# Attention's first 24 steps: where a unit of maxima stands in a step, and the queue of four early pairs of rows

## The chip, the cores and the metric

The kernel runs on one core of a Trainium2 chip. The metric is the time of one execution on the device, in microseconds. A core has five engines with an instruction queue each, which run in order and wait for each other through semaphores: TensorE (PE, matrix products; its weight loads are shown as PEld), VectorE (DVE), ScalarE (ACT), GpSimd (POOL) and SyncE (SP, which here only issues transfers). ACT and POOL can issue transfers too, from the same in-order queue that holds their arithmetic. [...]

## What is computed

Three stages follow each other: an attention in which a query sees only the keys of its own cluster, a dense layer pair, and a layer of eight experts. The change touches only the first:

```
q_assign = argmax(q_n . c_n)          # cluster of each query (and of each key, k_assign)
mask     = q_assign[:, None] == k_assign[None, :]
scores   = where(mask, scale * q @ k.T, -1e9)
scores   = scores - max(scores, axis=-1)
attn     = exp(scores) / (sum(exp(scores)) + 1e-9)
out      = attn @ v                   # batch 2, heads 8, sequence 768, head size 64
```

The heads are taken two at a time, so there are 8 pairs, numbered i from 0 to 7.

## The kernel before, in words

**Steps.** A pair of heads is 12 steps, in two halves r of 384 queries; there are 96 steps, called s0 to s95 here. `plan` (line 481) puts down for each step which functions are due in it, and `advance` (line 637) writes a step's instructions out. The order in which they are written is the order in each engine's queue.

**What a step holds.** `score` (line 385) makes the transposed scores of 128 keys and 384 queries for both heads: four matmuls on PE (lines 395 and 398) into one of two large PSUM tiles, then the exponential on ACT (line 402), which writes P. `pv` (line 418) multiplies the step before's P with the values: four matmuls (line 428). `add_up` (line 405) adds that P to a running sum on POOL, two additions (line 416). P has four buffers.

**Units of maxima.** The row maximum must be known before a half's scores are made. A unit (`max_unit`, line 355) is two matmuls of 96 rows (line 365) into a large PSUM tile and one reduction on DVE (line 369). A half of a pair has six units, 12 a pair: units 6 to 11 belong to pair 0's second half, 12 to 17 to pair 1's first, and so on. `RAMP` (line 552) places the early ones: steps 7, 9, 11, 17 and 20 have two units (14 and 15, 17 and 18, 20 and 21, 26 and 27, 30 and 31), steps 4 and 14 have none, and the others have one, as have all from step 24 on.

**The two large tiles.** `big` hands out two PSUM tiles in turn, to scores and units in the order in which they are written. A matmul into one of them waits until the instruction that read it last is through: the exponential of a score or the reduction of a unit.

**The small banks.** `misc` hands out three banks in turn to transposes of q and k (`split`, line 233), similarities to the centroids (`sims`, line 251), one-hot transposes (line 277), `first` (line 291), the sums (`norm1`, line 441), transposed maxima (`max_put`, line 374) and a part of the weights' narrowing (line 712). The bank of the sums is read last by `norm2`, one step after `norm1`, on DVE (line 456).

**max_put.** When a half's six units are done, `max_put` (line 371) transposes the maxima on PE, copies them on ACT (line 376, tile mt) and sends them with two transfers of 1.5 KB, one a head, into row 96 of QA, which the second matmul of `score` (line 398) reads. The pair of transfers is issued by SP, but for 0 < 2 i + r < 5, that is for the halves (0,1), (1,0), (1,1) and (2,0), by ACT (line 378). They are due in steps 4, 10, 14 and 20 and are needed by the scores of steps 6, 12, 18 and 24.

**The order within a step.** The first unit of the step comes ahead of all; then what was left late by the step before on DVE; then score, norm1, pv, add_up, onehot_t and first; then the rest (max_put, norm2 and norm3, split, sims, pick, spreads and loads on SP, narrowing); and last the step's second unit, if it has one:

```
for a in units[:1]:
    self.max_unit(*a)
```

With norm2, in the rest, POOL multiplies (line 455), DVE makes rs (line 456), ACT shifts it (line 464) and POOL multiplies again (line 465). norm1 of the halves (0,0), (0,1) and (1,0) is due in steps 8, 14 and 20, norm2 in steps 9, 15 and 21.

Of the kernel before, what the change touches and what calls it, by code (L numbers as in the profile page):

```python
# [23 lines left out]
def f32(ap):  # L24
    return ap.bitcast(F32)
# [144 lines left out]
class Attention:  # L170
# [200 lines left out]
    def max_put(self, i, r):  # L371
        nc, K, st = self.nc, self.K, self.st[i]
        pt = K.misc("pmt") if i + r else K.bank("a", "pmt")
        nc.tensor.transpose(pt[:, 0:128], self.mx[r], K.ident)
        mt = self.p.tile([6, 128], F32R, tag="mt", name="mt")
        nc.scalar.activation(out=mt, in_=pt[0:6, 0:128], func=AF.Copy, scale=-1.0)
        QA = self.QA[i % 3]
        e = nc.scalar if 0 < 2 * i + r < 5 else nc.sync
        for h in range(2):
            e.dma_start(  # L380
                out=f32(QA[96:97, h, 384 * r:384 * r + 384].rearrange("a (t p) -> a t p", t=3)),
                in_=f32(mt[3 * h:3 * h + 3, :]),
            )
# [97 lines left out]
    def plan(self, N):  # L481
# [5 lines left out]
        def at(s, f, *a):  # L487
            if s >= 0:
                steps.setdefault(s, []).append((f, a))
# [12 lines left out]
        for i in range(NP):  # L502
# [28 lines left out]
            if i:  # L531
                for j, kind in enumerate(("ql", "qu", "kb", "kl")):
                    for h in range(2):
                        at(max(12 * i - 12, 3) + self.BS * j, self.spread, i, (kind, h))
            if i:
# [8 lines left out]
                at(s, N.load, c + 3)  # L544
        return steps

    BS = 2
    SOON, SLOTS = (14, 19, 22), (0, 2, 7, 8, 10)
    B2 = 0

# [79 lines left out]
    def begin(self, C, Z, N):  # L630
        self.start(C, Z, N)
        self.steps = self.plan(N)
        self.late = []
        self.at = min(self.steps)
        self.end = max(self.steps) + 2

    def advance(self, upto, more={}):

        for s in range(self.at, upto):
            todo = self.steps.get(s, [])  # L640
            units = [a for f, a in todo if f == self.max_unit]
            first = [a for f, a in todo if f == self.max_put and a == (0, 1)]
            for a in units[:1]:
                self.max_unit(*a)
            for a in first:
                self.max_put(*a)
            for g in self.late:
                g()
            for g in more.get(s, []):
                g()  # L650
            now = (self.score, self.norm1, self.pv, self.add_up, self.onehot_t, self.first)
            todo = [x for f in now for x in todo if x[0] == f] + [x for x in todo if x[0] not in now]
            late = [f(*a) for f, a in todo if f != self.max_unit and not (f == self.max_put and a in first)]
            for a in units[1:]:
                self.max_unit(*a)
            self.late = [g for g in late if callable(g)]
        self.at = upto

# [1076 lines left out]
```

## Time and profile before

| | us |
|---|---|
| median of 3 runs | 788.06 (787.91 to 789.1) |
| the profiled execution | 787.98 |
| its span, first to last instruction | 786.1 |
| around the span | 1.9 |
| TensorE busy | 753.6 (96%) |
| VectorE busy | 588.8 (75%) |
| ScalarE busy | 466.6 (59%) |
| GpSimd busy | 220.7 (28%) |

Busy counts instructions that compute. An engine that issues a transfer is not counted as busy while it does so, and a matmul's end is modelled, so a row's start is surer than its end. Steps are recognised by the starts of line 395: s4 starts at 37.01 us, s5 at 40.81, s6 at 43.68, s7 at 46.43, s8 at 50.39, s9 at 53.19, s10 at 56.77, s11 at 59.47, s12 at 63.40, s14 at 67.73, s15 at 71.71, s16 at 74.78, s17 at 77.54, s18 at 81.51, s20 at 86.03, s21 at 90.16, s22 at 92.71 and s24 at 97.38.

### The profile page before, as it was taken

What the parts mean: (1) busy time and instruction counts of PE and PEld (TensorE: products, weight loads), DVE (VectorE), ACT (ScalarE), POOL (GpSimd) and SP (SyncE); (2) the same over time, 40 slices, a digit from 0 to 9 for tenths busy, and PEclk for the clock granted to TensorE, in tenths of its full rate; (3) what the DMA queues carried; (4) which work ended last, traced back from release to release, by engine and by line L of the source; (5) the groups of instructions that cost most, each with busy time, mean ns of one, the idle gap of its engine ahead of it and who ended that gap; (6) DMA issues with size and microseconds to landing.
All of it is one profiled execution on the core that took longest, in us unless ns stands there. A gap on an engine that the chain in (4) does not pass through costs nothing.

```text
span 786.1 us, 12515 instructions
## 1 busy us (share of the span) xinstructions
PE 753.6 (96%) x4295; PEld 607.5 (77%) x4297; DVE 588.8 (75%) x1195; ACT 466.6 (59%) x901; POOL 220.7 (28%) x247
## 2 busy tenths in 40 slices
PE   8989999999999989899999999999999999999994
PEld 5656566666654568788989899999888999999993
DVE  6756778879779799999997688788677665666661
ACT  4445778778776766555556454445645655656651
POOL 6256668787792200010000030000231101101110
PEclk9999999999999999999999999999999999999998
DMA  9696698989793539796465456232429867986640
GB/s 200 146 218 132 164 273 249 230 237 250 202 281 120 214 128 341 256 317 229 178 233 182 140 188 196 108 141 74 135 82 282 267 213 215 276 262 222 199 125 22
DMA packets 118694, 155.78 MB, mean 198 GB/s; under 512 B 35006, under 2 KB 82206, under 8 KB 114528
## 3 DMA queue, kind: packets, MB, share of 16 engines
q1 hardware_dynamic: 113952, 131.82, 57.6%
q0 software_dynamic: 4624, 23.09, 7.4%
q8 instruction: 36, 0.59, 0.3%
q14 instruction: 34, 0.28, 0.1%
q10 hardware_dynamic: 48, 0.01, 0.0%
HBM read 93.65 MB, written 42.24 MB: 173 GB/s over the span
## 4 chain that ended last, share of the span: by engine, by line
PE 70%; DVE 16%; issue 5%; ACT 4%; DMA 3%; POOL 1%; SPq 1%; ACTq 0%; POOLq 0%; DVEq 0%
PE ph L852 12%; PE o L913 11%; PE he L1509 9%; PE y L1542 9%; PE acc L428 6%; PE pm L365 4%; PE pst L395 3%; PE pst L398 3%; PE psim L251 3%; DVE m L369 2%; DVE n L867 2%; DVE cut L810 1%; DMA n<-in_moe_w_in_dram 1%; ACT r L877 1%; PE o L1161 1%
## 5 line engine op out<-in xcount | busy, mean ns | idle before, releaser
L810 DVE TENSOR_TENSOR cut<-raw,cut 128x512 fp32r<-128x512 f32 x168 | 110.1, 686 | 26.6 <-ACT cut L809 17.6
L369 DVE TENSOR_REDUCE m<-pm 128x1 f32<-128x768 f32 x96 | 91.0, 954 | 49.3 <-PE pm L365 48.9
L416 POOL TENSOR_TENSOR sum<-sum,P 128x384 f32<-128x384 f32 x104 | 104.3, 1034 | 13.1 <-ACT P L402 10.9
L402 ACT ACTIVATE P<-pst 128x768 f32<-128x768 f32 x96 | 77.7, 809 | 43.2 <-PE pst L398 40.4
L809 ACT ACTIVATE cut<-raw 128x512 fp32r<-128x512 f32 x168 | 98.1, 623 | 2.0 <-DMA raw<-in_moe_w_dram 2.0
L1542 PE MATMUL y<-cut,hy 128*128 128x512 f32 x384 | 99.3, 394 | 0.0
L1509 PE MATMUL he<-xeh,cut 128*128 128x256 f32 x512 | 92.5, 280 | 0.2 <-ACT xeh L1463 0.2
L877 ACT ACTIVATE r<-n,two 128x384 f32<-128x384 f32 x64 | 39.5, 617 | 81.1 <-DVE n L867 80.1
L1509 PEld LDWEIGHTS he<-xeh,cut 128*128 128x128 f32 x512 | 82.2, 188 | 5.5 <-ACT xeh L1463 0.4
L428 PE MATMUL acc<-P,vn 128*64 128x384 f32 x384 | 82.4, 508 | 0.1
L1542 PEld LDWEIGHTS y<-cut,hy 128*128 128x128 f32 x384 | 67.6, 188 | 10.9
L852 PE MATMUL ph<-xh,cut 128*128 128x384 f32 x256 | 67.1, 343 | 5.8 <-DVE t L889 3.5
L1509 PE MATMUL he<-xel,cut 128*128 128x256 f32 x256 | 71.5, 279 | 0.2 <-DVE xel L1464 0.2
L395 PE MATMUL pst<-QB,KB 128*128 128x384 f32 x192 | 67.1, 349 | 4.7 <-DVE m L369 3.5
L1514 ACT ACTIVATE hy<-he 128x256 fp32r<-128x256 f32 x64 | 24.5, 383 | 71.7 <-PE he L1509 71.7
L1554 POOL DMA_INDIRECT out_dram<-ye,meta x17 | 18.3, 1077 | 171.6 <-ACT ye L1552 156.9
L852 PE MATMUL ph<-xh,again 128*128 128x384 f32 x256 | 66.1, 339 | 0.0
L398 PE MATMUL pst<-QA,KA 97*128 97x384 f32 x192 | 64.9, 338 | 0.0
L913 PE MATMUL o<-cut,gh 128*128 128x512 f32 x192 | 59.8, 392 | 1.0 <-DVE rs L456 1.0
L1515 DVE SCALAR_TENSOR_TENSOR hy<-he,hy 128x256 fp32r<-128x256 f32 x64 | 27.1, 423 | 44.7 <-ACT hy L1514 44.7
L913 PE MATMUL o<-again,gh 128*128 128x512 f32 x192 | 59.6, 392 | 0.0
L365 PE MATMUL pm<-KA,QA 96*128 96x384 f32 x192 | 54.1, 369 | 2.8 <-DVE m L369 2.7
(238 smaller groups left out, 1616.1 us busy)
## 6 DMA issues: line engine op xcount, KB each, us to landing
raw<-in_moe_w_dram SPq DMA_DIRECT2D x72, 256.0 KB
raw<-in_moe_w_dram SPq DMA_DIRECT2D x36, 512.0 KB
kept<-cut POOLq DMA_DIRECT2D x16, 1024.0 KB, 8.5
again<-kept SPq DMA_DIRECT2D x16, 1024.0 KB
n<-in_moe_w_in_dram SPq DMA_DIRECT2D x16, 512.0 KB
n<-in_moe_w_out_dram SPq DMA_DIRECT2D x16, 512.0 KB
wf<-n SPq DMA_DIRECT2D x32, 256.0 KB
raw<-wf SPq DMA_DIRECT2D x16, 512.0 KB
```

The source lines that it names most:

```text
L365: nc.tensor.matmul(ps[:, g, 0:384], lhsT=QA[0:96, h, q0:q0 + 128], rhs=KA[0:96, h, 384 * g:384 * g + 384], start=True, stop=True,)
L369: nc.vector.reduce_max(out=self.mx[r][:, 3 * h + t:3 * h + t + 1], in_=ps[:, :, 0:384], axis=AX.XY)
L395: nc.tensor.matmul(ps[:, h, 0:384], lhsT=KB[:, h, ks], rhs=QB[:, h, qs], start=True, stop=False)
L398: nc.tensor.matmul(ps[:, h, 0:384], lhsT=KA[0:97, h, ks], rhs=QA[0:97, h, qs], start=False, stop=True)
L416: e.tensor_add(out=o[:, h], in0=a[:, h], in1=b[:, h])
L428: nc.tensor.matmul(acc[64 * h:64 * h + 64, 0:384], lhsT=st["v"][:, h, t, :], rhs=pt[:, h, :], start=(t == 0), stop=(t == self.NK - 1),)
L809: nc.scalar.activation(out=t[:, 0, part], in_=raw[:, part], func=AF.Copy)
L810: self.low.tensor_sub(out=t[:, 1, part], in0=raw[:, part], in1=f32(t[:, 0, part]))
L852: nc.tensor.matmul(ps[:, 0:384], lhsT=w[:, k, :], rhs=x[:, k, sl], start=(k == 0 and j == 0), stop=(k == 3 and j == 2),)
L913: nc.tensor.matmul(self.acc[t], lhsT=g[:, c], rhs=w, start=(f == 0 and j == 0), stop=(f == self.NF - 1 and j == 2),)
L1509: nc.tensor.matmul(ps[:, 0:MAIN], lhsT=w[:, k, :], rhs=x[:, k, :], start=(k == 0 and j == 0), stop=(k == 3 and j == 2),)
L1542: nc.tensor.matmul(st["y"][s], lhsT=g[:, c], rhs=w, start=(f == 0 and j == 0), stop=(f == 7 and j == 2))
```

## The change

In steps up to 23, from the first step with two units on (s7), a step's only unit is written behind score, norm1 and pv, and ahead of add_up, onehot_t, first and the rest. In a step with two, the first stays ahead of all and the second goes to that same place, where it was last of the step. From step 24 on nothing differs. Apart from this, the four pairs of transfers that ACT issued are issued by GpSimd.

```
-        e = nc.scalar if 0 < 2 * i + r < 5 else nc.sync
+        e = nc.gpsimd if 0 < 2 * i + r < 5 else nc.sync
...
-    BS = 2
+    BS, TURN = 2, 24
...
-        self.late = []
+        self.late, self.mid = [], False
...
-            for a in units[:1]:
+            self.mid = (self.mid or len(units) > 1) and s < self.TURN
+            ahead = units[:0 if self.mid and len(units) == 1 else 1]
+            for a in ahead:
                 self.max_unit(*a)
...
-            late = [f(*a) for f, a in todo if f != self.max_unit and not (f == self.max_put and a in first)]
-            for a in units[1:]:
+            todo = [x for x in todo if x[0] != self.max_unit and not (x[0] == self.max_put and x[1] in first)]
+            head = [x for x in todo if x[0] in (self.score, self.norm1, self.pv)]
+            late = [f(*a) for f, a in head]
+            for a in units[len(ahead):]:
                 self.max_unit(*a)
+            late += [f(*a) for f, a in todo if f not in (self.score, self.norm1, self.pv)]
             self.late = [g for g in late if callable(g)]
```

## Rows read from the trace of the kernel before

**Rows 1.** The page, part 1: span and PE's busy time.
```profile
span 786.1 us, 12515 instructions
...
PE 753.6 (96%) x4295; PEld 607.5 (77%) x4297; DVE 588.8 (75%) x1195; ACT 466.6 (59%) x901; POOL 220.7 (28%) x247
```
**Rows 2.** Groups of instructions on PE, 36.98 to 97.38 us (s4 to s23).
```profile
L395 PE MATMUL pst<-QB,KB 128*128 128x384 f32 x41 | 14.7, 359 | 4.3 <-DVE m L369 3.5 <-ACT P L402 0.8
...
L251 PE MATMUL psim<-cc,qh 128*128 128x256 f32 x12 | 3.4, 313 | 0.4 <-DVE rs L456 0.3 <-DVE n L734 0.2
```
**Rows 3.** Table by stretch: s7, s11, s14, s15, s16 and s22.
```profile
46.43:50.39 3.96, 3.26 (x19) 2.10 (x18) 2.13 (x4) 1.16 (x3) 1.97 (x2) 1.00 1.03 244
...
59.47:63.40 3.93, 3.16 (x18) 1.73 (x17) 3.05 (x5) 1.98 (x4) 3.26 (x5) 1.00 0.18 41
...
67.73:71.71 3.98, 3.81 (x24) 2.42 (x23) 1.92 (x3) 2.91 (x6) 3.73 (x4) 1.00 0.61 126
71.71:74.78 3.07, 2.81 (x18) 1.92 (x17) 1.59 (x3) 1.82 (x4) 1.64 (x3) 1.00 1.02 275
74.78:77.54 2.76, 2.76 (x18) 1.91 (x17) 2.39 (x4) 1.00 (x3) 2.76 (x4) 1.00 1.37 217
...
92.71:95.04 2.33, 2.33 (x15) 1.49 (x14) 2.09 (x4) 1.37 (x3) 2.30 (x3) 1.00 0.00 0
```
**Rows 4.** Timeline, PE and DVE, end of s7: units 15 and 16, then s8.
```profile
48.83 0.87 PE L365 MATMUL pm<-KA,QA 96*128 96x384 f32 x4
...
49.38 1.82 DVE L369 TENSOR_REDUCE m<-pm 128x1 f32<-128x768 f32 x2 [1.63 <-PE pm L365]
50.39 0.45 PE L395 MATMUL pst<-QB,KB 128*128 128x384 f32 x1 [0.70 <-DVE m L369]
```
**Rows 5.** Timeline, s4 and s5: ACT's transfers, its exponential, the next score.
```profile
37.85 2.00 ACTq L380 DMA_DIRECT2D QA<-mt  x2
...
39.95 0.81 ACT L402 ACTIVATE P<-pst 128x768 f32<-128x768 f32 x1 [2.13 <-PE psim L251]
...
40.81 0.45 PE L395 MATMUL pst<-QB,KB 128*128 128x384 f32 x1 [0.81 <-ACT P L402]
```
**Rows 6.** Timeline, DVE and PE in s15: the sum's last reader, the similarities.
```profile
72.95 0.55 DVE L456 SCALAR_TENSOR_TENSOR rs<-psum,rc 128x384 f32<-128x384 f32 x1
...
73.64 0.35 PE L251 MATMUL psim<-cc,qh 128*128 128x256 f32 x1 [0.26 <-DVE rs L456]
```
**Rows 7.** Timeline, DVE and PE in s21: the sum's last reader, then line 291.
```profile
91.41 0.54 DVE L456 SCALAR_TENSOR_TENSOR rs<-psum,rc 128x384 f32<-128x384 f32 x1
...
92.00 0.32 PE L291 MATMUL pp<-et,pre 128*64 128x384 bf16 x1
```
**Rows 8.** Timeline, DVE in s22: the narrowing behind a reduction.
```profile
94.31 0.68 DVE L725 SCALAR_TENSOR_TENSOR n32p<-n32p,n 128x512 int32<-128x512 int32 x1
```
**Rows 9.** Timeline, ACT in s10: the transfers of the half (1,0).
```profile
59.29 1.43 ACTq L380 DMA_DIRECT2D QA<-mt  x2
```
**Rows 10.** Timeline, POOL in s9 and s10.
```profile
56.67 1.00 POOL L465 TENSOR_TENSOR x<-x,rs 128x384 f32<-128x384 f32 x1 [1.33 <-ACT rs L464]
57.63 3.88 POOL L416 TENSOR_TENSOR sum<-sum,P 128x384 f32<-128x384 f32 x4
```
**Rows 11.** Line 814, GpSimd's own transfers (1 MB each, MoE stage): issue in ns, landing.
```profile
L814 POOL DMA_DIRECT2D kept<-cut x16: 531/533/792, 259.2 to 403.4; - x16
...
DMA to landing us min/median/max: 4.1/8.5/8.9
```
**Rows 12.** Timeline, POOL alone, MoE stage: the issue of one of these transfers.
```profile
285.84 0.58 POOL L814 DMA_DIRECT2D kept<-cut  x1 [9.73 <-DVE u L866]
```
**Rows 13.** DMA queues, 60.5 to 61.5 us (ACT's, q10) and 286.9 to 287.4 us (GpSimd's, q0).
```profile
q10 hardware_dynamic: 12, 0.00, 1.3%
...
q0 software_dynamic: 29, 0.24, 112.2%
```
**Rows 14.** Groups of instructions on POOL, 30 to 100 us.
```profile
L416 POOL TENSOR_TENSOR sum<-P 128x384 f32<-128x384 f32 x8 | 7.9, 1004 | 29.2 <-ACT P L402 29.2
```
## Prediction

> **What bounds the kernel now.** I read the page first: PE is busy 753.6 us of a span of 786.1 [rows 1], so a change is worth what it gives or takes of PE's idle time. Then the groups of PE from s4 to s23: line 395, the first matmul of a score, has 4.3 us of idle time before it, 3.5 behind a reduction of DVE and 0.8 behind ACT's exponential, and line 251 has 0.4 [rows 2]. That is nearly all that this stretch can give. The table by stretch prices PE's work where it hardly waits: s16 (score, pv, unit, similarities) takes 2.76 us, s22 (score, pv, unit, transpose) 2.33, both with PE busy throughout; s7 has 3.26 busy in 3.96, s11 3.16 in 3.93 [rows 3]. By the starts in the timeline a score costs 0.8 us of PE, a pv 0.8, a unit 0.44, so similarities cost 2.76 - 2.04 = 0.72 and a transpose 0.3; I estimate a one-hot transpose at 0.33 and s10's line 291 with max_put's transpose at 0.42.
>
> **The wait that the order makes.** At the end of s7 units 15 and 16 follow each other at once, and s8's score wants the large tile that unit 15 filled. The reductions start at 49.38, the score at 50.39, 0.70 us late [rows 4]. From the start of a unit to the score that takes its tile over lie 1.56 us (0.55 to the reduction, 0.96 for it, 0.05 to wake PE); the two units are 0.88 of it, and the rest stands still unless PE has something between the two. There are five such pairs of neighbours: units (15,16), (18,19), (21,22), (27,28), (31,32), 5 x 0.70 = 3.5 us, which is the 3.5 of the group [rows 2].
>
> **Part one, the order.** Writing the new order out, there are again five neighbours, others: (16,17), (19,20), (25,26), (29,30), (34,35). What lies between decides. Between 16 and 17 nothing does: s9's score waits 0.7, as s8's did. Between 19 and 20 lie line 291, max_put's transpose and a transpose of q (0.72): no wait. Between 25 and 26 lie similarities (0.72): none. Between 29 and 30 only the one-hot transposes (0.33): 0.4 is left. Between 34 and 35 a transpose (0.3): 0.4, up to 1.0, because in s22 and s23 DVE has the narrowing, about 0.7 apiece for two operations [rows 8], and a split's subtraction between reductions 33 and 34; I take 0.7. So the order removes 3.5 and leaves 0.7 + 0.4 + 0.7 = 1.8: **a gain of 1.7 us**.
>
> The reduction moves with its unit, and what stood behind it on DVE does too. In s15 the last similarities of pair 3 want the bank of the sums of half (0,1), which norm2's rs reads last. Before, unit 24 was first in the step, rs ran at 72.95 behind its reduction, and PE waited 0.26 [rows 6]. After, unit 24 comes behind score and pv (1.6 us into the step), its reduction starts 0.55 later and takes 0.96, and rs takes 0.55, so the bank is free 3.66 us into the step, while PE is there after 0.8 + 0.8 + 0.44 = 2.04. **PE waits 1.6 instead of 0.26: a loss of 1.4 us.** In s21 the same bank is wanted by line 291, which followed rs at 92.00, at once [rows 7]; by the same sum it now waits 1.6, of which about 0.1 was there: **a loss of 1.5 us.** In s9 rs moves behind reduction 18 too, but the bank's next user comes in s10: no cost to PE. ACT's line 464 and POOL's line 465 are late with rs; their cover is that norm3 uses x two steps later. Other waits on DVE stay as they were: the narrowing in s14, where no unit is due, holds PE for the same 0.2 as now [rows 2].
>
> **Part two, the queue.** ACT loses eight issues. Their first pair holds it 2.00 us from 37.85, so s4's exponential starts at 39.95, 2.13 after ACT's last work, and s5's score waits 0.81 for it [rows 5]. Without them the exponential follows the score's end: **a gain of 0.8 us**. The pair of s10 holds ACT 1.43 us [rows 9]; what PE lost by that lies in s11, whose wait of 0.7 is already counted. The pairs of s14 and s20 held up nothing of PE's that rows show: 0.
>
> POOL gains eight issues. A direct transfer of POOL's holds it 0.53 us (0.79 the first) [rows 11], so about 1.1 a pair. In s4 POOL has the maxima at once; three later additions shift by 1 us. In s14 and s20 it waits for max_put's copy with the next additions and both multiplications behind it; POOL's cover is the 29.2 us in which it sat idle before a half's first addition [rows 14], and norm1 takes the sum three steps later: 0. In s10 the pair stands behind line 465, which waits for ACT, and behind an addition pair: line 465 started at 56.67, the additions at 57.63 [rows 10], two of the four until 59.6. I find line 465 there again, since rs is late by as much as the steps are early. So the issues start at 59.6 instead of 59.29, while s12's score, which reads row 96, is ready some 2.5 us earlier than now, about 60.4 plus 0.5 for its last matmul.
>
> How soon does such a pair land? ACT's, issued at 59.29, had its twelve packets between 60.5 and 61.5 us [rows 13]. For POOL the trace has only 1 MB transfers: that of 285.84 [rows 12] had packets moving from 286.9 on [rows 13], so 1.1 from issue to first packet, and none landed before 4.1 [rows 11]. Ends: 1.1 + 0.4 and 4.1 from the second issue at 60.1. I take 1.6, the pair being tiny and the queues nearly empty then: landed at 61.7, **s12 waits 0.8 us** (0.3 to 3.3). For the pair of s4, issued under load, the same ends give s6 a wait of 0 to 1.0; I take 0.
>
> [...]
>
> **The sum.** Gains: 1.7 (order) + 0.8 (ACT) = 2.5. Losses: 1.4 (s15) + 1.5 (s21) + 0.8 (s12) = 3.7. Net 1.2 us slower. Behind s24 PE runs without waits at 2.33 or 2.76 a step [rows 3], so a shift is kept to the end. The profiled execution took 787.98, the median is 788.06; 787.98 + 1.2 = **789.2 us**. A measurement can tell some 0.2% (1.6 us) from no change, so this is no change by a little, on the slow side.
>
> **Rivals.**
> - A, *slower: the pairs come late over GpSimd.* If a small pair needs 4.1 us as the fastest of POOL's transfers did [rows 11], s12 waits 3.3 instead of 0.8 and s6 1.0 instead of 0: 789.2 + 3.5 = 792.7. For it: in s4 the engines are full, and half (1,0) has no room. Against: those were a thousand times larger. It decides once landing takes over 2 us. [...]
> - B, *faster: the banks do not bind.* Were the bank freed earlier, by line 446 or another reader, s15 and s21 would lose nothing: 789.2 - 2.9 = 786.3; with s12 unhurt as well 785.5. For it: a wait is put down to what came last, and PE's wait of 0.26 is small. Against: both instructions follow rs within 0.15 us.
> - C, *nothing comes of the order:* the neighbours keep their waits where fillers are held by banks themselves. Then 1.7 is lost: 790.9.
>
> **How the numbers follow.** Forecast (losses at the banks, short landing) 0.45, its own range 787.6 to 790.8; A 0.17; B 0.28; C 0.10. The range reaches into A and B: 785.4 to 792.2. Faster by over 0.2% (under 786.5): B, 0.28. Within: most of the forecast, 0.37. Slower (over 789.6): the rest of it, A and C, 0.35.
>
> **What would show it.** Right: PE's idle time before line 395 from s4 to s23 falls from 4.3 to about 2; line 251 in s15 and line 291 in s21 wait about 1.6 each behind rs; s5's score no longer waits for ACT; s12's second matmul waits for a transfer; s24 starts 1 to 2 us later than at 97.38. Wrong: s15 and s21 without such waits (B); s6 or s12 waiting over 2 us for row 96 (A); line 395 still idle 3.5 behind reductions (C).

## The result and the profile after

The changed kernel takes 794.24 us (median of 6 runs, 791.63 to 795.83) where the kernel before took 787.98 in the same session (6 runs). The ratio is 1.0071, with a 95% interval of 1.005 to 1.0093: **slower by 0.7%**. The forecast was 789.2 with a range of 785.4 to 792.2, so the sign was on its slow side and the size lies outside it.

The six executions differ in the clock that TensorE was granted over the span: 0.990 to 0.991 in the three slowest, 0.993 and 0.994 in two, 0.996 in the fastest, that of 791.63 us. The profiled one took 795.24 us, 1.0 above the median, at 0.991; the profiled one of the kernel before had 0.995. On its page (part 1: the span; busy time, share and instructions by engine) TensorE is busy 6.0 us longer than in [rows 1], with as many matmuls:

```profile
span 793.2 us, 12550 instructions
...
PE 759.6 (96%) x4297; PEld 609.5 (77%) x4297; DVE 590.3 (74%) x1195; ACT 466.3 (59%) x901; POOL 225.3 (28%) x255
```

So the loss is not only waiting. To see where it lies, take the steps by the starts of line 395. s4 starts 0.76 us later than before, which is the start of the program: the trace records a granted clock of 1.00 for TensorE from 7.05 us on instead of 4.03, and the first six transposes take 1.49 us instead of 0.84. The order doesn't set it: s4 starts at 36.80 us in e1 below, which has the same order, against 37.77 here, and the first pair on GpSimd is issued at 38.90. From s4 to s24 the stretch has grown by 5.28 us, from there to s95 by 0.1. Behind attention 0.3 is added at the start of the experts and about 0.65 in GpSimd's last instruction. Together 7.1, which is the difference of the spans (793.2 - 786.1).

The stretch from s4 to s24 in one row each, first the kernel before, then the changed one (columns: length, then busy time and count of PE, PEld, DVE, ACT, POOL, then the granted clock, DMA share, GB/s):

```profile
37.01:97.38 60.37, 55.48 (x309) 35.02 (x307) 37.60 (x60) 34.59 (x63) 38.83 (x40) 1.00 0.73 170
```
```profile
37.77:103.42 65.65, 60.58 (x308) 36.06 (x306) 39.11 (x61) 35.39 (x64) 45.61 (x50) 0.95 0.70 158
```

TensorE stands still 4.89 us in the first and 5.07 in the second, and it is busy 5.10 us longer with the same work. **The waits have only changed places; the loss is in the busy time.** Of that the clock explains a part: it is 0.95 here. The groups of PE in the stretch (busy time, mean ns of one | idle before, and on what) say where the waits went:

```profile
L428 PE MATMUL acc<-P,vn 128*64 128x384 f32 x80 | 18.5, 544 | 0.0
L395 PE MATMUL pst<-QB,KB 128*128 128x384 f32 x40 | 15.5, 387 | 0.8 <-DVE m L369 0.7
L398 PE MATMUL pst<-QA,KA 97*128 97x384 f32 x40 | 14.5, 363 | 0.1
L365 PE MATMUL pm<-KA,QA 96*128 96x384 f32 x48 | 14.2, 380 | 0.3 <-DVE m L369 0.3
...
L251 PE MATMUL psim<-cc,qh 128*128 128x256 f32 x12 | 3.6, 325 | 1.8 <-DVE rs L456 1.6 <-DVE n L739 0.2
...
L291 PE MATMUL pp<-et,pre 128*64 128x384 bf16 x4 | 1.4, 356 | 1.5 <-DVE rs L456 1.5
```

Against [rows 2], line 395 has 0.8 of idle time instead of 4.3 (another 0.65 stands before s24's own, just behind this window), and lines 251 and 291 have 3.3 where 251 had 0.4. The two new waits in the timeline (start, length, engine, operation, in brackets the idle time before it):

```profile
72.62 0.61 PE L365 MATMUL pm<-KA,QA 96*128 96x384 f32 x2
...
73.27 0.96 DVE L369 TENSOR_REDUCE m<-pm 128x1 f32<-128x768 f32 x1 [1.50 <-PE pm L365]
...
74.14 0.55 DVE L456 SCALAR_TENSOR_TENSOR rs<-psum,rc 128x384 f32<-128x384 f32 x1
...
74.84 0.35 PE L251 MATMUL psim<-cc,qh 128*128 128x256 f32 x1 [1.61 <-DVE rs L456]
...
95.66 0.37 PE L291 MATMUL pp<-et,pre 128*64 128x384 bf16 x1 [1.51 <-DVE rs L456]
```

This is the forecast's chain, in its order: unit, reduction, rs, and only then the bank is free. 0.48 us behind the end of the first wait, and 0.14 behind the second, the granted clock falls to 0.50 for 3.41 us (table by stretch, cut to the two falls):

```profile
75.32:78.73 3.41, 3.41 (x12) 1.80 (x11) 0.25 (x1) 1.08 (x3) 3.25 (x4) 0.50 1.25 258
...
95.80:99.21 3.41, 3.41 (x10) 1.63 (x10) 0.61 (x1) 1.79 (x3) 3.33 (x4) 0.50 0.17 31
```

TensorE is busy throughout both and gets through 12 and 10 matmuls. The kernel before has no such fall in this stretch: its clock is 1.00 over the whole of it (the first of the two rows above).

On the side of the queue, the exponential of s4 no longer stands behind transfers, and s5 starts without a wait (the timeline of s4 to s6 against [rows 5]):

```profile
38.84 0.81 ACT L402 ACTIVATE P<-pst 128x768 f32<-128x768 f32 x1 [0.26 <-PE pst L398]
38.90 1.35 POOL L380 DMA_DIRECT2D QA<-mt  x2 [1.76 <-ACT mt L376]
...
40.61 0.34 PE L395 MATMUL pst<-QB,KB 128*128 128x384 f32 x1
```

The chain of waits shows the other side: the second transfer of the pair landed 4.42 us after its issue began, and s6's last matmul of line 398, which reads that row 96, comes on its heels (start, length, what):

```profile
38.90 0.80 POOL QA L380
...
39.71 4.42 DMA QA<-mt
...
44.17 0.44 PE pst L398
```

s6 is 0.36 longer than before by that. In s12 the pair landed just in time: from the score's start to pv lie 1.08 us (62.45 to 63.53), where e1 below, which has the same order with the pairs on ScalarE, takes 0.88 (62.21 to 63.09). So about 0.2 is lost there. Over all eight transfers of line 380, GpSimd's issue takes 0.53 us and the landing 1.6 to 5.1, median 3.6.

### The profile page after: what moved, and what is told of

Same layout as the page of the kernel before. It is cut to its first block, busy times and chain, and to the rows that moved or that the text cites. A ratio compares the mean times of both kernels' runs of the same rounds, so it can differ in the third digit from the quotient of the medians.

```text
span 793.2 us, 12550 instructions
## 1 busy us (share of the span) xinstructions
PE 759.6 (96%) x4297; PEld 609.5 (77%) x4297; DVE 590.3 (74%) x1195; ACT 466.3 (59%) x901; POOL 225.3 (28%) x255
## 4 chain that ended last, share of the span: by engine, by line
PE 72%; DVE 16%; issue 5%; ACT 4%; DMA 2%; POOL 0%; POOLq 0%; SPq 0%; DVEq 0%; ACTq 0%
PE ph L857 12%; PE o L918 11%; PE he L1514 9%; PE y L1547 9%; PE acc L428 7%; PE pm L365 4%; PE pst L395 4%; PE pst L398 3%; PE psim L251 3%; DVE m L369 3%; DVE n L872 2%; DVE cut L815 1%; ACT r L882 1%; PE o L1166 1%; PE psum L441 1%
## 5 line engine op out<-in xcount | busy, mean ns | idle before, releaser
L365 PE MATMUL pm<-KA,QA 96*128 96x384 f32 x192 | 55.7, 373 | 3.2 <-DVE m L369 2.8
```

Of the source, the lines that this page charges most:

```text
L365: nc.tensor.matmul(ps[:, g, 0:384], lhsT=QA[0:96, h, q0:q0 + 128], rhs=KA[0:96, h, 384 * g:384 * g + 384], start=True, stop=True,)
```

## The experiments

Three questions: what do the two parts do alone, is it the waits in s15 and s21 that bring the clock down, and why does a removed wait of 3.5 us bring nothing even without them? One table for all that bears on the stretch. Length and busy time are of one profiled execution, from s4's start to s24's; "still" is the one less the other; e7's busy time holds the matmuls that it adds; the ratio is of all runs, to the kernel before on the same chip. (Where the order past s23 is changed too, or units are counted into another step, the stretch isn't comparable and is left out.)

| kernel | s4 to s24 | PE busy | still | falls of the clock | ratio, 95% interval |
|---|---|---|---|---|---|
| before | 60.37 | 55.48 | 4.89 | 0 | 1 |
| after | 65.65 | 60.58 | 5.07 | 2 | 1.0071 (1.005 to 1.0093) |
| e1: the order alone | 65.71 | 60.19 | 5.52 | 2 | 1.0067 (1.0054 to 1.008) |
| e2: the queue alone | 60.09 | 55.51 | 4.58 | 0 | 1.0021 (1.0012 to 1.003) |
| b3: the first pair sent later alone | 59.86 | 55.54 | 4.32 | 0 | 0.9991 (0.9982 to 1.0) |
| e8: one pair on GpSimd | 59.43 | 55.59 | 3.84 | 0 | 0.9995 (0.9986 to 1.0005) |
| e3: other banks in s15, s21 | 60.14 | 57.57 | 2.57 | 0 | 1.002 (1.0008 to 1.0032) |
| d1: other bank in s21 only | 62.94 | 59.16 | 3.78 | 1 | 1.0047 (1.003 to 1.0064) |
| e7: the two waits filled | 62.83 | 60.14 | 2.69 | 0 | 1.0045 (1.003 to 1.006) |
| e4: rs ahead of the unit | 60.95 | 57.37 | 3.58 | 0 | 1.0008 (0.9993 to 1.0022) |
| e5: e4, pairs on ScalarE | 60.59 | 57.35 | 3.24 | 0 | 0.9999 (0.999 to 1.0008) |
| b4: order to s13, pairs on ScalarE | 59.10 | 56.60 | 2.50 | 0 | 0.9985 (0.9976 to 0.9994) |
| c1: b4, first pair sent later | 58.55 | 56.75 | 1.80 | 0 | 0.9977 (0.9968 to 0.9985) |

**The order alone** (e1, the changed kernel with the pairs back on ScalarE).

```
-        e = nc.gpsimd if 0 < 2 * i + r < 5 else nc.sync
+        e = nc.scalar if 0 < 2 * i + r < 5 else nc.sync
```

> The change's order alone; the four pairs of transfers stay on ACT. Theory 1 (banks and clock): the waits of about 1.6 us behind rs in steps 15 and 21 are there, each followed by 3.4 us at a granted clock of 0.5, and s5's score waits for ACT's exponential as before, so the time is some 0.9 us above the full change, about 795. Rival (queue): the loss comes from the pairs on GpSimd; without them the time is 786 to 788. Rival (clock on its own): falls of the clock as in the full change, but at other places than behind the two waits.

793.35 us, 1.0067. Both falls are there, at nearly the same places (table by stretch of e1):

```profile
75.70:79.11 3.41, 3.41 (x12) 1.78 (x11) 0.63 (x2) 0.81 (x1) 3.41 (x5) 0.50 1.13 332
96.18:99.59 3.41, 3.41 (x12) 2.13 (x13) 1.04 (x2) 1.22 (x3) 3.41 (x5) 0.50 0.31 58
```

The loss belongs to the order; the queue hardly adds to it.

**The queue alone** (e2, the kernel before with this one line).

```
-        e = nc.scalar if 0 < 2 * i + r < 5 else nc.sync
+        e = nc.gpsimd if 0 < 2 * i + r < 5 else nc.sync
```

> The four pairs on GpSimd alone, in the order of before. Theory 1: s5's score starts about 0.9 us sooner, s6's and s12's may wait up to 0.5 us for row 96, no wait behind rs and no fall of the clock after the start: about 787.2, a gain of 0.5 to 0.9 us. Rival (queue): slower than before, 790 or more, with waits at s6 and s12.

789.83 us, 1.0021: slower, where a gain of 0.5 to 0.9 had been expected (in the prediction's sum this part comes to nothing: 0.8 gained in s5, 0.8 lost in s12). s5 gains its 0.96 us, and that is not kept. First, s6 waits for row 96, here visibly, and is 0.75 longer than before (timeline of e2):

```profile
37.90 1.35 POOL L380 DMA_DIRECT2D QA<-mt  x2 [1.76 <-ACT mt L376]
...
43.57 0.44 PE L398 MATMUL pst<-QA,KA 97*128 97x384 f32 x1 [0.47 <-DMA QA<-mt]
```

Second, 0.7 is lost up to s26, behind VectorE. Its line 477 takes 1.26 us where it took 0.56, while GpSimd is adding in both kernels (93.89 to 100.06 here, 93.71 to 99.88 before), and a unit waits for the reduction that comes later by it. Why line 477 took longer wasn't tried. The first row is of the kernel before, the others are of e2:

```profile
98.45 0.56 DVE L477 SCALAR_TENSOR_TENSOR xl<-x,xh 128x384 fp32r<-128x384 f32 x1
```
```profile
97.93 1.26 DVE L477 SCALAR_TENSOR_TENSOR xl<-x,xh 128x384 fp32r<-128x384 f32 x1
...
101.91 0.62 PE L365 MATMUL pm<-KA,QA 96*128 96x384 f32 x2 [0.32 <-DVE m L369]
```

Counted from s4, s95 stands 0.35 behind. Third, 0.3 is lost at the start of the experts and 0.65 at the very end. That the 0.3 comes from the queue isn't shown: from s95 to the start of the experts' last matmul into y lie 497.60 us in the kernel before and 497.88 in e2, but between 497.34 (b1) and 498.15 (e5) in kernels whose pairs are on ScalarE. The 0.65 is GpSimd's closing instruction, which the engine's own queue shows (count: shortest/median/longest ns, from first to last), first in e2, then in e1, which has no transfers of line 380 on GpSimd:

```profile
L1730 POOLq DRAIN  x3: 46/113/4401, 781.8 to 786.8; - x3
```
```profile
L1735 POOLq DRAIN  x3: 40/107/3752, 786.7 to 791.0; - x3
```

4401 ns with eight transfers more on the queue, 3752 without, as in the kernel before; the program ends with it.

**One pair of four** (e8, the kernel before with the pair of s4 alone on GpSimd) asks whether the gain of s5 can be had without the rest.

```
-        e = nc.scalar if 0 < 2 * i + r < 5 else nc.sync
+        e = (nc.gpsimd if 2 * i + r == 1 else nc.scalar) if 0 < 2 * i + r < 5 else nc.sync
```

> The order of before, and only the pair of half (0,1) on GpSimd, the other three on ACT. Theory: s5 0.96 us sooner, s6 waits 0.7 for row 96 as with all four pairs; the closing drain grows by a quarter of 0.65 us (about 3914 ns) if it goes by the number of transfers, or stays at 4401 if it is the first that counts: 787.9 to 788.5. Rival (the other three pairs cost POOL its additions): equal to the run with all four, 789.8.

The stretch is 0.94 shorter, but the median of 788.24 can't be told from before (788.69). The closing instruction takes 3911 ns: two transfers, 159 ns more. With 649 ns for eight that is some 80 ns for each transfer issued from GpSimd, paid at the end.

**Are the waits behind rs what brings the clock down?** In e3 the two instructions that waited take another bank; the order of all work stays.

```
+        if (i, nm, g) == (3, "q", 1):
+            K.nmisc += 1
...
+        if (i, g) == (3, 1):
+            K.nmisc += 1
```

> The full change, but the rotation of small banks skips one bank at the similarities of step 15 and at line 291 of step 21, so that neither needs the bank that rs reads; the order is unchanged. Theory 1: both waits of 1.6 us go and both falls of the clock with them: 794.2 - 3.1 - 3.4 = about 787.7. Rival (clock on its own): only the waits go, about 791. Rival (queue): about 794 still, or the waits move to other instructions.

Both waits and both falls are gone (table by stretch of e3, around the two places, and the whole stretch):

```profile
73.00:78.00 5.00, 5.00 (x32) 3.60 (x30) 3.56 (x7) 1.70 (x4) 4.39 (x6) 1.00 1.27 242
92.00:99.00 7.00, 6.07 (x32) 3.45 (x32) 5.91 (x9) 5.44 (x10) 6.92 (x8) 1.00 0.46 105
...
37.46:97.60 60.14, 57.57 (x309) 34.74 (x307) 38.69 (x61) 34.80 (x64) 43.95 (x48) 1.00 0.76 173
```

5.5 us of the stretch come back, 789.91 us in all; of what still lies above the kernel before, 0.65 is the queue's, at the end as in e2, and 0.4 lies in the experts, where the kernels scatter by as much. In **d1** only the second of the two edits is made, so that s15 waits and s21 does not.

> The full change, but line 291 of step 21 takes another small bank, so that the wait behind rs is left in step 15 alone. Theory (each wait brings its own fall of the clock, and a fall costs about 1.4 us beside the wait's 1.5): one fall, at 75 us, none at 96, and about 2.9 us less than the full change, 791. Rival (a fall needs both waits, or the second follows from the first): none, 788, or both, 793.

One wait, one fall (74.54 to 77.95), none near 96; the stretch is 2.80 us longer than e3's and 2.71 shorter than the changed kernel's. In these profiles each wait brings its own fall, and wait and fall cost 2.8 us together, where the forecast had 1.4 and 1.5. Other executions, of which there is no profile, differ: d1's six lie between 790.04 us at a granted clock of 0.995 and 794.42 at 0.990, and one of e3's, at 793.43, has 0.990 without either wait.

In **e7** the waits are left and filled: six matmuls of zeros into a free bank, whose result nothing uses, stand ahead of each of the two instructions.

```
+        if (i, g) == (3, 1):
+            K.nmisc += 1
+            t = K.misc("warm")
+            for _ in range(6):
+                nc.tensor.matmul(t, lhsT=K.idle[:, 0:128], rhs=K.idle, start=True, stop=True)
+            K.nmisc += 1
```

> The full change, with six matmuls of zeros (128 x 512, bf16) into a free small bank just ahead of the similarities of step 15 and of line 291 of step 21; nothing else is computed with them. The waits behind rs stay, but PE works through most of each. Theory (the clock falls because PE stands still): no fall of the clock at 75 and 96 us, s16 and s22 start as in the full change, and the time is 3.4 us less, about 790.8. Rival (the falls come of something else): they stay, about 794.

The bank still sets the start (0.20 us of idle time is left before each, timeline of e7), but no fall follows (table by stretch):

```profile
92.67 1.47 PE L300 MATMUL warm<-idle 128*128 128x512 bf16 x5
...
94.34 0.32 PE L303 MATMUL pp<-et,pre 128*64 128x384 bf16 x1 [0.20 <-DVE rs L468]
```
```profile
75.30:79.00 3.70, 3.70 (x24) 2.62 (x23) 1.19 (x3) 1.53 (x4) 3.25 (x4) 1.00 1.20 264
...
92.00:99.00 7.00, 6.75 (x33) 3.59 (x33) 4.05 (x6) 4.06 (x8) 6.91 (x8) 1.00 0.26 65
```

So in s15 and s21 it is TensorE's standing still that the falls follow, not the late bank. By the lengths of the stretch the waits alone cost 2.7 us (e7's 62.83 less e3's 60.14), the two falls 2.8 (65.65 - 62.83), that is 1.4 each; 3.4 had been expected. The changed kernel's one execution at 0.996, 791.63 us, lies close to e7's median of 791.92.

**Why is nothing gained without the waits?** e3 stands still 2.3 us less than the kernel before and yet gains 0.2: its 309 matmuls take 57.57 us instead of 55.48, at a granted clock of 1.00 in both. The same holds for **e4**, where norm2 is added to what comes ahead of the late unit, so that rs is not delayed, and **e5**, which is e4 with the pairs on ScalarE.

```
+            ahead_of = (self.score, self.norm1, self.pv, self.norm2)
...
-            late += [f(*a) for f, a in todo if f not in (self.score, self.norm1, self.pv)]
+            late += [f(*a) for f, a in todo if f not in ahead_of]
```

> The full change, but norm2 is written ahead of the step's late unit, so that rs runs before the reduction. Theory 1: the same as with the other bank, about 787.7, perhaps 0.3 less or more because the reduction is 0.5 us later and norm2's multiplications on GpSimd come ahead of the additions. Rival (clock on its own): about 791.

> The new order with norm2 ahead of the late unit (as in the run before), the pairs on ACT. Theory (banks and clock for the order; for GpSimd's queue a late row 96 in s6, and a longer closing drain of POOL, 4401 ns where kernels without the pairs have 3752, and some 0.4 us at the start of the experts): s5 waits for ACT again (+0.9), s6 no longer waits (-0.3 to -0.7), the drain is 3752 ns again (-0.65), the experts -0.4: about 788.1, equal to the kernel before within 0.1%. Rival (GpSimd's queue costs nothing after attention): about 789.2.

Neither has a fall in the stretch, both are level with the kernel before (788.61, 788.44), and both have PE busy some 1.9 us longer than it. e4's pair over GpSimd was the latest of all: s6 waited 1.3 us for it.

**e6** keeps the new order through all of attention (e5 with 200 for 24 as the step where it ends).

```
-    BS, TURN = 2, 24
+    BS, TURN = 2, 200
```

> As e5, but the late place of the unit holds to the end of attention (TURN 200), so that units 34 and 35 are not neighbours and no score of s24 waits. Theory: the turn at step 24 cost the order 1.0 to 1.5 us (from s22 to s24 the run with the other bank lost 1.9 us against before), so about 786.9. Rival: in the later steps DVE's narrowing behind the late reductions makes waits of its own at each step, and the time is above 789.

796.96 us, 1.0095. The turn at s24 costs nothing now, but from there the kernel falls back by about 0.115 us a step: its distance to the kernel before grows by 2.3 us from s40 to s60. (From s60 to s88 it grows by 6.7, in which lies a fall of the clock, 6.83 us long, at 255.) Nothing waits in these steps. Two steps of the same content, a transpose of q or k in each, show what grows. The kernel before, timeline of PE:

```profile
192.60 0.55 PE L233 MATMUL pt<-ident,kn 128*128 128x128 f32 x3
192.90 0.59 PE L365 MATMUL pm<-KA,QA 96*128 96x384 f32 x2
193.33 0.34 PE L395 MATMUL pst<-QB,KB 128*128 128x384 f32 x1
193.51 0.34 PE L398 MATMUL pst<-QA,KA 97*128 97x384 f32 x1
```

and e6:

```profile
193.39 0.62 PE L365 MATMUL pm<-KA,QA 96*128 96x384 f32 x2
193.85 0.49 PE L233 MATMUL pt<-ident,qn 128*128 128x128 f32 x3
194.09 0.42 PE L395 MATMUL pst<-QB,KB 128*128 128x384 f32 x1
194.35 0.34 PE L398 MATMUL pst<-QA,KA 97*128 97x384 f32 x1
```

From a score's first matmul to its second lie 0.18 us behind a unit and 0.26 behind a transpose; the rest of the step is as long in both orders (1.53 and 1.50 from pv to the next score), and the whole step takes 2.39 instead of 2.32. In e3 it is 0.28 behind one-hot transposes, and a unit ahead of one-hots or of line 291 takes 0.55 instead of 0.46. **What a product cost here depended on what stood before it on TensorE.** The whole of the 2.1 us can be counted in this way: added up from start to start, without idle time, the matmuls of the stretch take 55.48 us in the kernel before and 57.57 in e3, so it isn't an effect of the modelled ends. The largest part, 0.9, lies between the first and the second matmul of a unit: 0.18 behind similarities or another unit (thirteen of 24 units before, five in e3), 0.28 behind pv (two before, sixteen in e3). 0.3 lies between a score's first and second, where the old order had a unit between the small bf16 or transposing matmuls and the score, and the rest in the distances between other neighbours. A unit of the kernel before behind similarities, ahead of a score, then one of the changed kernel behind pv, ahead of one-hots, 0.36 and 0.55 us to the next start:

```profile
43.32 0.52 PE L365 MATMUL pm<-KA,QA 96*128 96x384 f32 x2
43.68 0.34 PE L395 MATMUL pst<-QB,KB 128*128 128x384 f32 x1
```
```profile
55.26 0.62 PE L365 MATMUL pm<-KA,QA 96*128 96x384 f32 x2 [0.31 <-DVE m L369]
55.81 0.52 PE L277 MATMUL pe<-identb,e 128*64 128x128 bf16 x6
```

Why a matmul takes longer behind such a neighbour wasn't tried.

**b2** ends the new order at s28 instead of s24 (e5 with 28).

```
-    BS, TURN = 2, 24
+    BS, TURN = 2, 28
```

> As the run with norm2 ahead and the pairs on ACT, with the turn at step 28 alone. Theory: 1.3 us less than with the turn at 24, about 787.2. Rival (the loss at s22 to s24 is the narrowing behind late reductions, wherever the turn): no less than 788.4.

s24 comes 1.24 us earlier against s0 than in e5 (0.44 of it is a unit that now stands behind s24's products), and steps 24 to 40 give 0.84 of it back: 787.92 us, 0.9994 (0.9985 to 1.0003). **b4** goes the other way and ends it at s14; the pairs are on ScalarE, and norm2 stands where the change had put it. The second units of s17 and s20 then still come right behind pv.

```
-    BS, TURN = 2, 24
+    BS, TURN = 2, 14
```

> The new order as the change has it, but up to step 13 alone (step 14 has no unit), pairs on ACT. Theory: two of three neighbours' waits of 0.7 us go before s14 and one is left, nothing is late behind rs in s15 and s21, the clock doesn't fall: 0.4 to 0.6 us less than before. Rival (the order loses in every step): the same or slower.

787.26 us, 0.9985: faster. PE is busy 1.1 us longer than before in the stretch instead of 2, and stands still 2.4 less. No unit is late in a step with rs and a wanted bank.

**The pair of s4 on ScalarE, but later.** What the change wanted from the other queue, an exponential that doesn't wait, can be had by issuing the pair behind that exponential (b3, on the kernel before).

```
+        def send():
+            for h in range(2):
+                e.dma_start(
...
+        if (i, r) != (0, 1):
+            return send()
+        self.send = send
...
+                if f == self.score and first:
+                    self.send()
```

> The order of before, ACT's pair of half (0,1) issued behind s4's exponential instead of ahead of it. Theory (the issue held ACT, and that alone kept s5's score): s5 0.95 us sooner and nothing else moved, about 787.6 beside 788.6. Rival: s6 waits for row 96, which now lands about 0.9 us later, and the gain is gone by s7.

s5 comes 0.96 earlier, s6 waits 0.5 for row 96: 787.61 us, 0.9991 (0.9982 to 1.0), at the edge of what can be told. **b1** has it together with e5's order up to s27.

> The new order with norm2 ahead of the late unit, the turn at step 28 instead of 24 (similarities lie between the two neighbouring units there, and no narrowing falls in steps 27 to 29), all four pairs on ACT, but that of half (0,1) issued behind s4's exponential. Theory: no wait behind rs, no fall of the clock, s5 about 0.95 us sooner, no extra wait at the turn (1.3 us), POOL's drain at 3752 ns: about 786.3, faster than both kernels. Rival: s6 waits for row 96, or the steps 24 to 27 lose what the turn saved: 787.5 to 788.5.

787.69 us, 0.9993 (0.9984 to 1.0002): no more than either alone. (The profile is of its slowest execution, 790.15 us.) **c1** has it together with b4's order:

> The two edits that gained most, together: the new order to step 13, and ACT's pair of half (0,1) issued behind s4's exponential (pairs on ACT). Theory: they free different waits of PE, s5's and two of those before s13, so the gains add, less what s6 waits for row 96 (0.5 us): 787.3 - 0.5 = about 786.8 beside a before of 788.4. Rival: the earlier steps make s6 and s12 wait for row 96, and nothing is added.

786.70 us (11 runs, 786.04 to 787.9) against 788.51 in the same session: 0.9977 (0.9968 to 0.9985), faster than both kernels and the best of the study.

## Why the prediction was wrong

**Right.** The two banks: 1.61 us in s15 and 1.51 in s21, where 1.6 was worked out for each, and e3 shows that the bank is the reason. ScalarE's freed exponential: s5 0.96 us earlier, 0.8 forecast. The wait that the order moves to s9: 0.70, as long as the one of s8 that it replaces [rows 4]. The turn at s24: 0.65 where 0.7 was taken. Rivals B and C fall: the banks bind, and line 395 does lose its waits, 3.5 us of them in the stretch.

**Small terms.** In s20, 0.4 was left by the sum and hardly anything by the chip: s19 is busy 3.21 of its 3.26 us, and its one-hot transposes, put at 0.33 without a row, take 0.45 (87.46 to 87.91); in s9, 0.3 before a unit that the sum didn't have. s12 was to wait 0.8 for row 96 and lost about 0.2; the 0.4 from the first packet to the landing in that term was an estimate, and no run shows it: the eight transfers here landed 1.6 to 5.1 us after the issue; s6 was to wait nothing, "I take 0", and is longer by 0.36 here, by 0.75 in e2 and by 1.6 in e4. Rival A had the right mechanism for s6 and the wrong step for its weight. With all of this TensorE stands still 0.2 us more than before, where the forecast's sum came to 1.2; its terms were off in both directions. That PE runs without waits behind s24 can't be read from [rows 3], which end with s22, and a unit waits 0.32 at 164.59; the shift was kept all the same, within 0.1.

**The first step that failed** is the price of the two waits, "PE waits 1.6 instead of 0.26: a loss of 1.4 us" and "a loss of 1.5 us". It took a wait for its length. Behind each the granted clock went to half for 3.41 us, which cost 1.4 us more each time (after less e7; d1 shows that they come one by one). That is 2.8 us, and no term or rival had it, though the sum itself put the longest standstills of the whole stretch into s15 and s21.

**The second step that failed** is the way in which PE's work was priced, "By the starts in the timeline a score costs 0.8 us of PE, a pv 0.8, a unit 0.44": as if each had one price wherever it stands. With the units behind pv, the same 309 matmuls take 2.1 us longer (e3 against before), which eats "a gain of 1.7 us" whole. The unit at 0.44 is an example: behind pv and ahead of one-hots it takes 0.55.

**The third** is what was left out: GpSimd's closing instruction, 0.65 us for eight transfers, which e2 has and e1 has not. Another 0.3 at the start of the experts isn't shown to be the change's.

Put together from s4 to s24, standing still 0.2, neighbours 2.1 (as in e3), clock 3.0 (the 5.1 of busy time less the 2.1) make 5.3, as measured. That the sign was right on the slow side is partly luck: of the 2.9 us put on the banks' waits 2.7 is there (e7 against e3), but the gain of the order that should have paid for more than half of it is not. The execution of 791.63 us even lies inside the stated range, with the neighbours' 2.1 us that the sum didn't have.

## What to carry to other kernels

Look at what the clock does behind a new wait of the bottleneck engine: here two standstills of TensorE of 1.5 to 1.6 us cost nearly twice their length in the profiled executions, and filling them with useless matmuls, or better giving the waiting instruction another buffer, got half or all of that back. It is a risk and not a rule; a longer standstill in b1, of 2.33 us, brought no fall (below). When instructions are moved on a full TensorE, compare the start-to-start times of the pairs of neighbours that the new order makes, not the mean of each kind. A transfer that is moved to another queue takes its issue, its landing and the queue's closing with it: on GpSimd here 0.53 us of issue, 1.6 to 5.1 us to the landing and some 80 ns at the end for each.

## What the runs showed of the hardware

**The clock.** TensorE's granted clock fell to 0.50 for 3.41 us behind each standstill of 1.5 to 1.6 us at s15 and s21, in the changed kernel, e1 and (once) d1, though TensorE was busy 3.46 of 3.63 us in the step ahead of the first, and all of the 3.26 us ahead of the second. It did not fall behind the five waits of 0.70 of the kernel before [rows 2, 4], nor in e4 behind one of 1.35 in s6. Length alone doesn't decide: later in attention b1 has a standstill of 2.33 us without a fall (timeline, then table by stretch, up to its end and from there):

```profile
242.13 0.62 PE L365 MATMUL pm<-KA,QA 96*128 96x384 f32 x2 [2.33 <-DVE m L369]
```
```profile
238.00:242.20 4.20, 1.87 (x11) 0.83 (x9) 4.20 (x3) 2.61 (x6) 2.79 (x3) 1.00 0.04 9
242.20:246.00 3.80, 3.70 (x20) 2.50 (x20) 3.73 (x7) 2.32 (x4) 0.32 (x1) 1.00 0.18 69
```

e6 has one of 1.65 us that ends at 247.19, and its clock stays at 1.00 until 255.01, behind two more of 1.11 and 0.42 (the mean over its span is 0.990). b3's clock falls at 249.69, at the end of a standstill of 1.16 (the mean over its span is 0.993); the kernel before stands still 1.14 us at the same place (to 250.29) and has no fall. What decides between such cases was not found.

**GpSimd's small transfers.** 1.5 KB landed 1.6 to 5.1 us after the issue in the changed kernel, and the pair of s4 made s6 longer by 0, 0.36, 0.75 and 1.6 us in e8, the changed kernel, e2 and e4.
